# A fused recurrence and long-convolution kernel: the input matrix loaded raw and transposed by transfers, its factor moved to the output matrix, exponentials on ScalarE, and a fixed order of all operations

## The chip, the cores and the metric

The kernel runs on one core of a Trainium2 chip. The metric is device time in microseconds (us) of the core; a time exceeds the profile's span by about 2 us. Engines are named as the profile names them: PE is TensorE's matmuls, PEld its weight loads, DVE is VectorE, ACT is ScalarE, POOL is GpSimd, SP is SyncE.

Every run is called fast or slow: slow when it is more than 1.5% above the fastest run of the same kernel in its round. Ratios use fast runs only. A profile is one execution.

## The reference

Two independent parts, written side by side into one output of 2048 rows and 1280 columns, bfloat16.

```python
# A: a diagonal complex recurrence, 640 states, 2048 steps
dt = exp(log_dt); Lam = Lambda_re + 1j*Lambda_im
Lam_bar = exp(dt * Lam)
B_bar = ((Lam_bar - 1) / Lam)[:, None] * (B_re + 1j*B_im)     # the factor G times B
h[t] = Lam_bar * h[t-1] + B_bar @ x[t]
y[t] = 2 * real(C @ h[t]) + x[t] * Dskip
# B: a short convolution of k with 4 taps, times v, then a long convolution
kv = (short convolution of k along time) * v                   # 2048 x 640
y = irfft(rfft(kv, 4096) * rfft(ssm_k, 4096))[:2048] + kv * ssm_D
out_B = q * y
```

The recurrence is linear in its input, so the factor `(Lam_bar - 1) / Lam` may be applied to B, as the reference writes it, or to C.

## The kernel before

The program is a list of 700-odd named operations, each with an estimated cost on every engine that may run it. A list scheduler inside the kernel's file picks the order at build time: among the ready operations it takes the one that can start first by its own cost figures, with a due time to break ties.

```python
class Graph:
    SEM = 0.12
    ...
    def schedule(self, slots, ordered_tags, free_tags):
        ...
        while len(out) < n:
            best = None
            for o in ready:
                ...                                   # buffers free? engines free?
                for e, c in o.alts.items():           # every engine that may run it
                    ...
                    cand = (s, o.due, fin, o.idx, o, e, c, pick, td)
                    if best is None or self.better(cand, best, free):
                        best = cand
```

The powers of part A's start: e to the power of an argument is taken on GpSimd. `rn` holds the moduli of seven powers of `Lam_bar`, and the factor, the sets (`M_n`, block-diagonal 128-wide matrices made from them) and B's product all follow from it.

```python
        small("dtb", lambda: g.tensor_tensor(out=dt_b[:], in0=ecol[:, 0, :], in1=lpar[:, 0, :], op=ALU.pow), ["lam", "nrowf"], ["dt_b"], 0.4, "POOL")
        ...
        small("rn", lambda: g.tensor_tensor(out=rn[:], in0=ecol[:], in1=rn[:], op=ALU.pow), ["nrho"], ["rn"], 0.6, "POOL")
```

B is multiplied by the factor's set and so also transposed, in 50 products ("bb"). The large products ("dn", the bulk of part A) then take x against it, at full width. C is transposed by 100 products against an identity ("ct").

```python
            def f(e, blk=blk, pt=pt):                       # bb
                P = self.P(pt)
                for q, (j, k) in enumerate(blk):
                    self.nc.tensor.matmul(P[:, q // 4, 128 * (q % 4):128 * (q % 4) + 128],
                                          lhsT=bv(j // 5)[:, j % 5, 128 * k:128 * k + 128], rhs=self.mgv()[:, j, :], start=True, stop=True)
            ...
            def f(e, b=b):                                  # dn
                P = self.P(pt)
                for k in range(5):
                    nc.tensor.matmul(P[:, b, :], lhsT=self.BbT[:, j, k, :], rhs=self.xT[:, k, hf, 2 * b:2 * b + 2, :]
                                     .rearrange("p s m -> p (s m)"), start=(k == 0), stop=(k == 4))
```

Part B goes in five groups of 128 columns. For each, k and v come by DMA transposes on SyncE, the short convolution runs on VectorE, its result goes out to memory ("kvs") and is read back in another layout ("kvl", tile `kvd`), then two product stages, a pointwise part, two inverse stages ("i2", "i1") with one SBUF-to-SBUF transpose ("zt") between them, and the multiplication by q ("ob").

## Time and profile before

| | before |
|---|---|
| time | 249.55 us median of 3 runs (249.28 to 251.15) |
| span of the profile | 247.7 us |
| PE busy | 197.6 us, 80% |
| DVE busy | 181.0 us, 73% |

The first lines of the page: the span, busy time with its share, and the span in 40 slices of 6.2 us, each digit a busy share in tenths. PEclk is the clock that TensorE was granted, as far as the trace has records of it: they begin at 33.2 us here, and PEclk reads full up to its first record.

```profile
span 247.7 us, 8544 instructions
...
PE 197.6 (80%) x3843; PEld 139.3 (56%) x3857; DVE 181.0 (73%) x283; ACT 134.0 (54%) x164; POOL 37.6 (15%) x52
...
PE   0001688799999999889999749689979998999593
...
PEclk9999999999999999999999976999999999999999
...
```

PE does nothing in the first three slices, and is nearly full from 50 us on. The one dip that PEclk shows (slices 23 and 24, counted from 0) goes with the dip of PE in slices 22 and 23.

What PE waited for, the longest first (line of the waiting product, what released it: us in all, times, longest):

```profile
...
PE ps L672 <- DVE s L445: 21.2, 2, 20.9
PE ps L957 <- issue: 3.5, 2, 3.2
PE ps L1087 <- DMA s<-s: 3.0, 1, 3.0
...
```

What VectorE waited for, and the operation it waited for (the tile view: its duration in ns, then its start in us):

```profile
...
DVE rc L393 <- POOL rn L365: 10.2, 1, 10.2
...
```

```profile
...
L365 POOL TENSOR_TENSOR rn<-ecol,rn x1: 11567/11567/11567, 7.9 to 7.9; 128x70 f32<-128x70 f32 x1
...
```

Read together: the first useful products (line 672, B by its factor) start 20.9 us late. The wait names a VectorE operation, but VectorE itself stood still for 10.2 us, until one GpSimd power of 11.6 us was done. The first large product in the timeline (start, duration):

```profile
...
37.64 2.10 PE L702 MATMUL ps<-xT,BC 128*128 128x512 bf16 x8
```

Busy time of each engine by stretch (us, with the number of instructions):

```profile
...
core 0: us, PE busy (x) PEld busy (x) DVE busy (x) ACT busy (x) POOL busy (x), PEclk, DMA share, GB/s
0.00:24.00 24.00, 0.75 (x6) 0.61 (x7) 10.19 (x53) 4.24 (x8) 21.52 (x29) 1.00 0.88 178
24.00:50.00 26.00, 20.19 (x484) 16.67 (x485) 25.37 (x37) 22.96 (x26) 4.52 (x5) 1.00 0.84 159
50.00:90.00 40.00, 39.48 (x651) 23.54 (x653) 37.26 (x55) 25.16 (x34) 0.71 (x2) 1.00 0.58 114
...
```

From 24 to 90 us VectorE is nearly full (25.37 of 26, 37.26 of 40), and PE has done 20.9 us of work by 50 us. The groups of the large products and of B's products (count, busy us, mean ns):

```profile
...
L702 PE MATMUL ps<-xT,BC 128*128 128x512 bf16 x186 | 45.9, 380 | 1.5 <-ACT s L249 0.7
...
L672 PE MATMUL ps<-s,s 128*128 128x128 bf16 x50 | 4.8, 261 | 21.4 <-DVE s L445 21.2
...
```

14 of the 200 large products have no record in this trace, so their busy time is a little more than it shows.

### The profile page before, as it was taken

Reading aid. Unit: us, or ns where it says so; the run is one execution under the profiler, and the core shown is the slowest. Engines: PE = TensorE matmul, PEld = TensorE weight load, DVE = VectorE, ACT = ScalarE, POOL = GpSimd, SP = SyncE. Lnnn points to the kernel's source line nnn. Section 1 sums busy time; section 2 is a strip of 40 time slices with the busy share of each in tenths; the row PEclk is TensorE's granted clock in tenths of the full one; section 3 lists DMA queues with packets and bytes.
Section 4 is the critical chain, followed back from the end, with each engine's and each line's share of the span. In section 5 each row is a group of like instructions: output and inputs, shape, how many; then the busy total and the mean of one; then the engine's idle time right before and its main releaser. Section 6 shows DMA issues by size and latency. Waiting matters only on the chain.

```text
span 247.7 us, 8544 instructions
## 1 busy us (share of the span) xinstructions
PE 197.6 (80%) x3843; PEld 139.3 (56%) x3857; DVE 181.0 (73%) x283; ACT 134.0 (54%) x164; POOL 37.6 (15%) x52
## 2 busy tenths in 40 slices
PE   0001688799999999889999749689979998999593
PEld 0001575655655765547555628567757775777472
DVE  5408999999999899998868968763999557661110
ACT  2400999796674367775466746555257516652121
POOL 8896010500000010000011100001030110000000
PEclk9999999999999999999999976999999999999999
DMA  5997599494019496487494990554769494006414
GB/s 152 227 180 139 123 192 194 129 204 95 4 21 232 109 174 150 86 116 199 107 210 100 257 224 26 156 81 110 176 165 156 160 208 103 29 29 140 112 56 111
DMA packets 86695, 33.73 MB, mean 136 GB/s; under 512 B 82018, under 2 KB 84450, under 8 KB 86658
## 3 DMA queue, kind: packets, MB, share of 16 engines
q1 hardware_dynamic: 84916, 26.72, 55.3%
q0 software_dynamic: 1712, 6.46, 10.2%
q8 instruction: 30, 0.49, 0.8%
q14 instruction: 7, 0.06, 0.1%
q10 hardware_dynamic: 30, 0.00, 0.0%
HBM read 12.47 MB, written 7.86 MB: 82 GB/s over the span
## 4 chain that ended last, share of the span: by engine, by line
PE 57%; DVE 18%; POOL 7%; DMA 6%; ACT 6%; issue 4%; SPq 0%; DVEq 0%; ACTq 0%; POOLq 0%
PE ps L854 16%; PE ps L702 13%; PE ps L993 7%; PE ps L957 6%; DVE s L1016 5%; PE ps L1087 5%; POOL rn L365 5%; DMA s<-s 3%; DVE s L932 3%; DMA s<-in_B_k_dram 3%; ACT s L249 2%; DVE s L926 2%; PE ps L1049 2%; PE ps L803 2%; PE ps L858 2%
## 5 line engine op out<-in xcount | busy, mean ns | idle before, releaser
L249 ACT CAST s<-ps 128x1024 bf16<-128x1024 f32 x79 | 76.8, 1021 | 25.8 <-PE ps L993 12.0
L702 PE MATMUL ps<-xT,BC 128*128 128x512 bf16 x186 | 45.9, 380 | 1.5 <-ACT s L249 0.7
L854 PE MATMUL ps<-BC,hb 128*128 128x320 bf16 x240 | 36.4, 300 | 0.0
L251 DVE CAST s<-ps 128x1024 bf16<-128x1024 f32 x21 | 25.5, 1223 | 12.9 <-PE ps L993 8.1
L249 ACT CAST yo<-ps 128x640 bf16<-128x640 f32 x16 | 11.1, 692 | 37.3 <-PE ps L858 28.9
L957 PE MATMUL ps<-R,s 64*64 64x128 bf16 x1280 | 24.5, 228 | 6.8 <-issue 3.5
L702 PEld LDWEIGHTS <-BC 128*128 128x128 bf16 x200 | 18.8, 98 | 19.9 <-issue 1.0
L957 PEld LDWEIGHTS <-s 64*64 64x64 bf16 x1280 | 21.0, 113 | 12.9 <-issue 12.3
L854 PEld LDWEIGHTS <-hb 128*128 128x128 bf16 x240 | 21.9, 98 | 8.6
L1016 DVE TENSOR_TENSOR s<-s,s 128x1024 bf16<-128x1024 bf16 (+1 forms) x30 | 25.0, 866 | 0.8 <-DVE s L251 0.2
L993 PE MATMUL ps<-s,Wre 128*64 128x128 bf16 x320 | 22.4, 231 | 2.2 <-ACT s L249 1.8
L993 PEld LDWEIGHTS <-Wre 128*64 128x64 bf16 x320 | 19.4, 116 | 8.0 <-issue 6.3
L807 DVE TENSOR_TENSOR hb<-ps,hb 128x512 bf16<-128x512 f32 x30 | 19.6, 685 | 5.8 <-PE ps L803 5.7
L1094 DVE TENSOR_TENSOR s<-ps,s 128x1024 bf16<-128x1024 f32 x10 | 12.0, 1219 | 15.5 <-PE ps L1087 15.1
L249 ACT CAST hb<-ps 128x768 bf16<-128x768 f32 x19 | 15.3, 805 | 14.2 <-PE ps L702 12.8
L993 PE MATMUL ps<-s,Wim 128*64 128x128 bf16 x320 | 22.1, 228 | 0.0
L672 PE MATMUL ps<-s,s 128*128 128x128 bf16 x50 | 4.8, 261 | 21.4 <-DVE s L445 21.2
L993 PEld LDWEIGHTS <-Wim 128*64 128x64 bf16 x320 | 19.6, 116 | 0.0
L932 DVE TENSOR_TENSOR s<-s,s 128x2048 bf16<-128x2048 bf16 x15 | 18.4, 1224 | 0.4
L672 PEld LDWEIGHTS <-s 128*128 128x128 bf16 x50 | 4.2, 118 | 21.8 <-issue 21.8
L926 DVE TENSOR_SCALAR s<-s,sk 128x2048 bf16<-128x2048 bf16 x20 | 14.8, 750 | 0.4
L1087 PE MATMUL ps<-Ct,s 128*64 128x64 bf16 x640 | 12.3, 200 | 3.0 <-DMA s<-s 3.0
(156 smaller groups left out, 291.4 us busy)
## 6 DMA issues: line engine op xcount, KB each, us to landing
s<-kvd SPq DMA_DIRECT2D x5, 512.0 KB, 4.1
out_dram<-s SPq DMA_DIRECT2D x10, 256.0 KB, 4.1
out_dram<-yo SPq DMA_DIRECT2D x14, 160.0 KB, 2.9
s<-in_B_ssm_k_dram POOLq DMA_DIRECT2D x4, 512.0 KB, 7.0
kvd<-s SPq DMA_DIRECT2D x4, 512.0 KB, 2.6
s<-in_B_q_dram SPq DMA_DIRECT2D x6, 256.0 KB, 5.1
s<-in_B_q_dram POOLq DMA_DIRECT2D x4, 256.0 KB, 5.3
s<-in_A_x_dram SPq DMA_DIRECT2D x1, 960.0 KB, 5.3
```

What stands on the lines that cost most here:

```text
L249: self.nc.scalar.copy(out=out, in_=in_)
L251: self.eng[e].tensor_copy(out=out, in_=in_)
L365: small("rn", lambda: g.tensor_tensor(out=rn[:], in0=ecol[:], in1=rn[:], op=ALU.pow), ["nrho"], ["rn"], 0.6, "POOL")
L702: nc.tensor.matmul(P[:, b, :], lhsT=self.BbT[:, j, k, :], rhs=self.xT[:, k, hf, 2 * b:2 * b + 2, :] .rearrange("p s m -> p (s m)"), start= ...
L807: v.tensor_tensor(out=hv(r), in0=self.P(p2)[:, 0, :].rearrange("p (h m) -> p h m", h=2), in1=hv(r), op=ALU.add)
L854: nc.tensor.matmul(P[:, part, 0:320], lhsT=hap(j), rhs=self.CT[:, j, c0:c0 + 320], start=(j == 0), stop=False)
L926: v.tensor_scalar_mul(out=out, in0=k(j), scalar1=self.sk[:, G, j:j + 1])
L932: op(f"ca{j}{G}{h}", {"DVE": dve_tt(W_)}, lambda e, c=c, tt=tt: v.tensor_tensor(out=c(), in0=c(), in1=tt(), op=ALU.add), r=[f"tm{G}{h}"], ...
L957: nc.tensor.matmul(P[64 * ri:64 * ri + 64, r, 128 * b4:128 * b4 + 128], lhsT=d[64 * r:64 * r + 64, 4 * qd + b4, a0, :], rhs=self.R[64 * r: ...
L993: nc.tensor.matmul(P[64 * pi:64 * pi + 64, ri, 128 * k4:128 * k4 + 128], lhsT=W[:, kp, pi, :], rhs=A[:, kp + 16 * pi, :], start=True, stop ...
L1016: v.tensor_tensor(out=o, in0=a, in1=b, op=op_)
L1087: nc.tensor.matmul(P[64 * ah:64 * ah + 64, b // 8, 64 * (b % 8):64 * (b % 8) + 64], lhsT=Z[:, 16 * h + b, 64 * ri:64 * ri + 64], rhs=self. ...
```

## The change

Three things at once. The powers become exponentials on ScalarE, with one more load of the sine table placed early. B is loaded by four DMA transposes and used raw; the factor is applied to C, which comes by four DMA transposes too. And the scheduler is replaced by a fixed order with fixed engines for all operations, which a search over the whole program had found. The intent: the large products need only x and B, so they can start before the phases are ready, and the order fills what follows better.

```diff
-    SEM = 0.12
+    SEM = 0.06
@@ the order @@
+    def place(self, slots, text):
+        letter = {"P": "PE", "A": "ACT", "D": "DVE", "G": "POOL", "S": "SP"}
+        ...
+        for word in text.split():
+            name, _, e = word.partition("/")
+            o = ops[name]
+            o.eng = letter[e] if e else next(iter(o.alts))
+            ...
+ORDER = """
+ld_ldt ld_lre J0 consts J1 ... px1 ci1 ss ex0/A px2 px3 ex1/D px4 ex2/A dtap1/D s1h12
+ex3/A set_1_0/D B10 s1h10 set_3_0/D e1h12/A set_2_0/G s1h11 ... dn1_8_0 kvl0/G e1h03/A ... cv310/D q0/G ...
+... (721 names in all)
+"""
-        order = self.g.schedule({"8": self.N8, "4": self.N4, "P": 4, "Y": 2}, ("8", "4"), ("P", "Y"))
-        return order
+        self.slots = {"8": self.N8, "4": self.N4, "P": 4, "Y": 2}
+        return self.g.place(self.slots, ORDER)
@@ the exponentials @@
-        small("dtb", lambda: g.tensor_tensor(out=dt_b[:], in0=ecol[:, 0, :], in1=lpar[:, 0, :], op=ALU.pow), ["lam", "nrowf"], ["dt_b"], 0.4, "POOL")
+        small("dtb", lambda: s.activation(out=dt_b[:], in_=lpar[:, 0, :], func=ACT.Exp), ["lam"], ["dt_b"], 0.3, "ACT", due=-24)
-        small("rn", lambda: g.tensor_tensor(out=rn[:], in0=ecol[:], in1=rn[:], op=ALU.pow), ["nrho"], ["rn"], 0.6, "POOL")
+        def f_rn():
+            s.activation(out=rn[:], in_=rn[:], func=ACT.Exp)
+            s.activation(out=scr[:], in_=self.hpi[:], func=ACT.Sin)
+        small("rn", f_rn, ["nrho", "hpi"], ["rn"], 1.8, "ACT", due=-22)
@@ B raw: the 50 products and their evictions go; the large products at half width @@
+                    nc.sync.dma_start_transpose(out=self.BT[:, :, u, 320 * h:320 * h + 320], ...
-                    nc.tensor.matmul(P[:, b, :], lhsT=self.BbT[:, j, k, :], rhs=...)
+                    for ri in range(2):
+                        nc.tensor.matmul(P[64 * ri:64 * ri + 64, b, :], lhsT=self.BT[:, k, ri, 64 * j:64 * j + 64], rhs=...)
@@ C: 100 products against the identity become 40 against the factor's set @@
-                        nc.tensor.matmul(P[64 * h:64 * h + 64, q // 4, ...], lhsT=cv(h)[:, k, 64 * j:64 * j + 64], rhs=self.ident[:], ...)
+                            nc.tensor.matmul(self.P(pt)[:, u, 0:320], lhsT=self.M["G"][us, 2 * J + ri, :],
+                                             rhs=cv(ri)[us, J, 320 * b:320 * b + 320], start=(ri == 0), stop=(ri == 1))
@@ engines: sets may run on POOL, the convolution's scalings on ACT @@
-            mk_set(n, lambda i=i: ss[:, i, :, :], ["ss"], {"DVE": 0.85})
+            mk_set(n, 10, lambda i=i: ss[:, i, :, :], "ss", {"DVE": 0.85, "POOL": 2.2}, 2)
... (cost figures, signs of the sets, small tiles reused: left out)
```

In the order, a letter after the slash is the engine (A ScalarE, D VectorE, G GpSimd, S SyncE).

## The prediction

> **What bounds the kernel now.** The page's busy table gives PE 197.6 of 247.7 us (80%), DVE 181.0 (73%), ACT 134.0 (54%). Busy time by stretches shows three regimes:
> - 0 to 24 us: PE busy 0.75 us. The chain of waits runs through POOL: dt_b (2.0 us), then `rn`, a power on 128x70 elements that takes 11.57 us; DVE idles 10.2 us for it (waits view). Then come the factor, its set, W and the products of B. The first large product (line 702) starts at 37.6 (timeline).
> - 24 to 112 us: DVE is full (25.4 of 26, 37.3 of 40, 20.9 of 22); from 93 to 112 the chain lies mostly on DVE.
> - After 112: PE leads, with about 19 us of its idle time left: an issue gap of 3.2 us at 142, the second coarse step at 154 to 162, a transpose landing in 7.6 us at 224, the tail.
>
> PE work at its back-to-back pace in the timeline (5 of 512 columns 1.08 us; a half row of projection 1.5; 16 stage-two products 0.5; and so on) adds up to only about 181 us.
>
> **What changes.**
> 1. Both powers leave POOL (13.6 us in the chain). Instead: two exponentials on ACT (estimate 0.26 us each, as its other 70-wide operations) and two more table loads, 1.28 us each in the trace. [...] The phase chain should end near 12 us instead of 19.5.
> 2. The 50 products of B with its factor (3.4 us) and their 7 evictions go; B comes by four transposes (about 2.7 us of queue each, estimated from x's 16.1 us for 8). Large products then need only x and B: the first at 17 to 18 us instead of 37.6. C's 100 products (3.5 us) become 40, about 2.7 us; altogether 14 evictions (13 us) become 10 of 640 columns (0.69 each, 7 us).
> 3. Large products become 400 half-width ones instead of 200. Stage two (128x64) runs 64 of 128 columns in 1.98 us, 31 ns each, so pairs run side by side; I expect a pair of 512 columns to keep 216 ns. [...]
> 4. Some sets move to POOL, a few scalings (estimate 1.9 us against 0.75) to ACT; DVE's total stays near 180 us.
> 5. The fixed order spreads the projections between B's stages and puts 10 us of other PE work behind the last transposes.
>
> **Sum.** At 50 us, before has done about 16 us of dense PE work: a lag of 34. After should reach its first large product with a lag of 12: 20 us off the start on PE, though DVE's lag falls only from 14 to 7. PE: 12 lag + 181 dense with switches + 15 holes (PE and DVE are now equally loaded, and a fixed order slips) + 4 tail = 212 span; times exceed the span by 1.8.
>
> Predicted **214 us**, range **207 to 226**. Chances: faster 0.97, same 0.02, slower 0.01.
>
> **Signs.** The exponential under 0.5 us on ACT; first large product before 20 us; PE busy near 190 us, above 87% of the span; large products near 45 us busy in all (not 85); DVE above 80%; the late transpose wait gone.
>
> **What would make it wrong.** Half-width pairs not overlapping (+40 us); transposes slowed by other traffic, so that x's second half comes after 45 us; [...] holes of 25 us rather than 15 (about 225), or nearly none (about 205).

The sum came to 212 us of span, 214 of time. "With switches" stands for 1 to 2 us that I added for changes between forms of product, a cost that no trace shows.

## The result, and the profile after

| | before | after |
|---|---|---|
| time, same chip | 249.42 us median of 4 runs (249.04 to 251.15) | 237.49 us median of 4 runs (232.37 to 244.95) |
| fast runs | | 232.37, 232.81 |
| slow runs | | 242.17, 244.95 |
| span of the profile | 247.7 us | 230.8 us (a fast run) |
| mean granted clock of the profile, from its first record on | 0.986 | 0.963 |

A ratio is the mean time of one kernel's fast runs over that of the other's of the same rounds, so it is not quite the ratio of the medians above. Here it is 0.931 (95% interval 0.924 to 0.939): faster, but by 6.9%, not 14%, and half of the runs are slow ones. The median of 237.49 us lies outside the range on record, and so do the fast runs.

The same lines of the page, after:

```profile
span 230.8 us, 8736 instructions
...
PE 195.7 (85%) x3947; PEld 137.3 (59%) x3947; DVE 180.8 (78%) x279; ACT 140.7 (61%) x166; POOL 44.1 (19%) x67
...
PE   0619996979999999997659999659999999999953
...
PEclk9976999999999999999988999958999999999999
...
```

PE has work from slice 1 on (transposes of x), a hole in slice 2, and 9 tenths in slice 3, where it had 1 tenth before. It is busy for 1.9 us less in all. PEclk now has three dips, at slices 2 and 3, 20 and 21, and 26 and 27.

The exponentials in ScalarE's timeline (start, duration, line, operation):

```profile
...
8.37 0.21 ACT L430 ACTIVATE dt_b<-lpar 128x10 bf16<-128x10 f32 x1
9.17 0.26 ACT L445 ACTIVATE rn<-rn 128x70 f32<-128x70 f32 x1 [0.58 <-DVE rn L442]
9.43 1.28 ACT L446 ACT_TABLE_LOAD   x1
...
```

Both exponentials take under 0.3 us, and the table load 1.28 us, as predicted. The first large product, and the large products as a group:

```profile
...
20.89 1.49 PE L751 MATMUL ps<-xT,BC 128*64 128x512 bf16 x12
```

```profile
...
L751 PE MATMUL ps<-xT,BC 128*64 128x512 bf16 x400 | 47.4, 381 | 0.2 <-ACT s L331 0.2
...
```

400 products at half width have a mean of 381 ns and take 47.4 us of busy time, where 186 of the 200 at full width took 45.9: pairs of them run side by side, as predicted. The stretches, and what PE waited for:

```profile
...
core 0: us, PE busy (x) PEld busy (x) DVE busy (x) ACT busy (x) POOL busy (x), PEclk, DMA share, GB/s
0.00:24.00 24.00, 11.44 (x201) 9.07 (x203) 20.51 (x55) 14.57 (x22) 15.90 (x31) 0.86 1.04 194
24.00:50.00 26.00, 22.92 (x382) 13.17 (x378) 23.62 (x43) 19.30 (x25) 10.02 (x10) 1.00 1.06 181
50.00:90.00 40.00, 39.33 (x729) 24.57 (x728) 34.09 (x52) 29.74 (x35) 1.75 (x3) 1.00 0.56 100
...
```

```profile
...
PE ps L1132 <- DMA s<-s: 6.9, 4, 4.3
PE ps L1002 <- DVE s L924: 4.3, 1, 4.3
PE ps L703 <- DMA s<-in_A_x_dram: 4.1, 2, 3.9
PE ps L1002 <- issue: 2.7, 2, 2.2
...
```

PE has done 34.4 us of work by 50 us, 13.4 more than before. It had been meant to be about 22 further (a lag of 12 for one of 34). The 6.9 us of waits for line 1132 are inverse steps waiting for the transposes of their input, and one of them has a second price:

```profile
...
core 0: us, PE busy (x) PEld busy (x) DVE busy (x) ACT busy (x) POOL busy (x), PEclk, DMA share, GB/s
...
148.00:152.00 4.00, 0.03 (x1) 0.00 (x0) 1.78 (x2) 0.48 (x1) 0.00 (x0) 0.83 1.24 189
152.00:156.00 4.00, 3.68 (x71) 2.77 (x72) 1.19 (x2) 0.00 (x0) 0.00 (x0) 0.50 0.71 218
...
```

PE stood still from 148.0 to 152.3 us, and then worked at half clock (PEclk 0.50) until 157.5. Such stretches follow three holes (13.0 to 17.3, 118.4 to 120.6 and 148.0 to 152.3 us). A product takes about twice as long in them: ten of line 899 took 2.87 us at 154.6 us and 1.52 at 157.7, just after the third. So I count half of the busy time in them as lost: 1.8, 1.4 and 2.6 us, 5.8 in all, where the kernel before lost 3.1 after its one hole. In the trace's clock records the three stretches lasted 6.83, 3.41 and 6.83 us, and in the third PE was busy for 1.72 of the first 3.41 us and for all of the second. How long a hole it takes, and what ends a stretch, is not shown: the clock fell at 119.9 us, where PE had been busy for 1.47 of the 3.41 us before, and stayed whole after a wait of 2.2 us in r1_after_again.

PEclk misses a part of it, because the trace's clock records begin late. Products of one form (128 columns on the full array), in the timeline of the kernel before, on either side of its first record at 33.2 us (start, duration, count at the end):

```profile
...
23.79 1.87 PE L672 MATMUL ps<-s,s 128*128 128x128 bf16 x16 [20.85 <-DVE s L445]
...
33.18 1.52 PE L632 MATMUL ps<-ident,s 128*128 128x128 bf16 x24
...
```

That is 117 ns each, then 63 (107 and 56 from start to start). In the changed kernel the change from 107 to 55 lies between 10.3 and 12.4 us, and its first record is at 10.7. So I count PE's busy time up to the first record as half clock too: 7.3 us before (3.6 lost) and 4.2 after (2.1 lost). With these, half clock cost PE 6.8 us before and 7.8 after, and its work at full clock is 190.8 and 187.9 us.

One identity makes every profile comparable. With the PE work done by 50 us, the PE work in all, and PE's idle time after 50 us, read from the stretches,

span = (50 - work by 50) + work in all + idle after 50.

| kernel (profile) | span | 50 - PE busy by 50 us | PE busy in all | PE idle after 50 us |
|---|---|---|---|---|
| before | 247.7 | 29.1 | 197.6 | 21.1 |
| prediction | 212 | 12 | 181 | 19 |
| after | 230.8 | 15.6 | 195.7 | 19.4 |

So, of the 16.9 us that the fast profile gained, 13.4 come from the start, 1.9 from less PE time and 1.6 from fewer holes.

The prediction's row is in another unit, though: its lag and its 181 count dense work, at full clock. (It gives the kernel before a lag of 34, where this table has 29.1.) In its unit, with what half clock cost after 50 us put to the last column, the identity reads:

| kernel (profile) | span | 50 - full-clock work by 50 us | full-clock work in all | idle, or lost to half clock, after 50 us |
|---|---|---|---|---|
| before | 247.7 | 32.7 | 190.8 | 24.2 |
| prediction | 212 | 12 | 181 | 19 |
| after | 230.8 | 19.5 | 187.9 | 23.4 |
| r3_exp_only | 254.7 | 33.2 | 188.9 | 32.6 |
| r3_new_greedy | 249.8 | 25.9 | 191.9 | 31.9 |
| r4_loads_sp_again | 227.2 | 18.5 | 187.0 | 21.7 |
| r4_pow_back | 236.3 | 27.2 | 186.9 | 22.3 |
| r4_sets_dve | 227.3 | 18.2 | 186.5 | 22.6 |

The change gained 13.2 us at the start, 2.9 of PE work and 0.8 after 50 us. The miss of 18.8 us against the predicted span is 7.5 at the start, 6.9 of PE work and 4.4 of holes and half clock: all three terms were too small. In the four profiles of the fixed order in this table (the kernel after and three of the r4 runs) the work is nearly constant (186.5 to 187.9 us), while PE's busy time runs from 193.0 to 197.5: that difference is nearly all half clock.

### The profile page after: what moved, and what is told of

It reads as the page before. It is cut to its first block, busy times and chain, and to the rows that moved or that the text cites. A ratio compares the mean times of both kernels' runs of the same rounds, so it can differ in the third digit from the quotient of the medians.

```text
span 230.8 us, 8736 instructions
## 1 busy us (share of the span) xinstructions
PE 195.7 (85%) x3947; PEld 137.3 (59%) x3947; DVE 180.8 (78%) x279; ACT 140.7 (61%) x166; POOL 44.1 (19%) x67
## 5 line engine op out<-in xcount | busy, mean ns | idle before, releaser
L331 ACT CAST s<-ps 128x1024 bf16<-128x1024 f32 x81 | 78.4, 1020 | 26.0 <-PE ps L1002 12.9
L751 PE MATMUL ps<-xT,BC 128*64 128x512 bf16 x400 | 47.4, 381 | 0.2 <-ACT s L331 0.2
L899 PE MATMUL ps<-BC,hb 128*128 128x320 bf16 x240 | 38.1, 307 | 1.9 <-issue 1.7
L751 PEld LDWEIGHTS <-BC 128*64 128x64 bf16 x400 | 21.5, 110 | 18.0 <-issue 2.0
L899 PEld LDWEIGHTS <-hb 128*128 128x128 bf16 x240 | 22.6, 100 | 12.4 <-issue 2.4
L333 DVE CAST s<-ps 128x1024 bf16<-128x1024 f32 x19 | 22.8, 1220 | 6.0 <-PE ps L1002 4.4
L331 ACT CAST yo<-ps 128x640 bf16<-128x640 f32 x11 | 7.6, 691 | 28.8 <-PE ps L903 19.3
L1038 PE MATMUL ps<-s,Wre 128*64 128x128 bf16 x320 | 21.1, 221 | 0.4 <-issue 0.2
L331 ACT CAST hb<-ps 128x768 bf16<-128x768 f32 x17 | 13.5, 798 | 8.0 <-PE ps L751 8.0
L1132 PEld LDWEIGHTS <-s 128*64 128x64 bf16 x640 | 11.7, 117 | 10.1 <-DMA s<-s 7.6
L912 POOL DMA_DIRECT2D out_dram<-yo x6 | 3.4, 573 | 72.5 <-ACT yo L331 37.3
L1061 DVE TENSOR_TENSOR s<-s 128x1024 bf16<-128x1024 bf16 x20 | 13.8, 688 | 0.3
```

The source lines that it names most:

```text
L331: self.nc.scalar.copy(out=out, in_=in_)
L333: self.eng[e].tensor_copy(out=out, in_=in_)
L751: nc.tensor.matmul(P[64 * ri:64 * ri + 64, b, :], lhsT=self.BT[:, k, ri, 64 * j:64 * j + 64], rhs=self.xT[:, k, hf, 2 * b:2 * b + 2, :].re ...
L899: nc.tensor.matmul(P[:, part, 0:320], lhsT=hap(j), rhs=self.CT[:, j, c0:c0 + 320], start=(j == 0), stop=False)
L1038: nc.tensor.matmul(P[64 * pi:64 * pi + 64, ri, 128 * k4:128 * k4 + 128], lhsT=W[:, kp, pi, :], rhs=A[:, kp + 16 * pi, :], start=True, stop ...
L1061: v.tensor_tensor(out=o, in0=a, in1=b, op=op_)
```

## The experiments

Sixteen runs. All results were correct. The records call the theories by letters in places: A is the half clock after holes, B that the clock falls for another cause, E is a clash of two GpSimd-issued loads with transposes.

### First round: the state, the clock, the start

**r1_after_again**: no edit, the changed kernel once more on the chip of this round.

> The changed kernel once more, as the yardstick for the three runs beside it. Fast runs near 232.6 us as before; if the slow runs (242 and 245 us at granted clocks of 0.94 and 0.92) are a property of this kernel, some of these will be slow again; if they were an accident of the first chip, none will.

Measured: 238.9 us median of 6 runs: 228.23 and 229.8 at one end, 242.69, 244.07 and 244.66 at the other, and 235.11 between them. Ratio of the fast runs 0.918 (0.910 to 0.925). So the kernel has two states by itself, some 14 us apart, and more slow than fast runs. In its profile (fast, 227.7 us) the wait for the transposes at 147.8 us was 2.2 us instead of 4.3, and no half clock came after it.

**r1_warm_filler**: 18 useless products ahead of the inverse step `i120`, in the PSUM tile it overwrites, to keep PE busy in the hole.

```diff
+                if G == 2 and h == 0:
+                    for _ in range(18):
+                        nc.tensor.matmul(P[:, 0, :], lhsT=self.ident[:], rhs=self.xT[:, 0, 0, 0:2, :]..., start=True, stop=True)
```

> Only 18 useless products of 512 columns are put in front of the late-transpose products of the third group, into the same PSUM tile that those products overwrite, so that TensorE has work in the 4.3 us in which it waits for that transpose (148.0 to 152.3 us in the profile). Theory A [...]: no half-clock stretch at 151 to 157.7 us, 2.5 to 3 us less time, about 229.8 us against 232.6. Theory B [...]: the half-clock stretch stays or moves, time the same within 0.5 us or longer.

Measured: 242.15 us median (236.89 to 244.86); the profile fell in a slow run. The clock stayed whole after the fillers, but the time can't be judged: no run was near the fast state. What the slow profile gave is where a slow run parts from a fast one. PE waited for the reload of the first group's convolution result:

```profile
...
PE ps L1004 <- DMA s<-kvd: 6.7, 1, 6.7
...
```

(after, fast: 0.7 us at that place). Two stretches of the fast profile of the changed kernel, with the transfers' share and GB/s in the last columns, and then the same two stretches of the slow run:

```profile
...
core 0: us, PE busy (x) PEld busy (x) DVE busy (x) ACT busy (x) POOL busy (x), PEclk, DMA share, GB/s
...
48.00:52.00 4.00, 2.69 (x113) 1.92 (x117) 1.92 (x3) 1.77 (x3) 0.00 (x0) 1.00 0.98 182
52.00:56.00 4.00, 3.90 (x121) 3.24 (x111) 3.96 (x5) 2.99 (x4) 0.00 (x0) 1.00 0.64 135
...
```

```profile
...
48.00:52.00 4.00, 0.61 (x10) 0.22 (x4) 1.23 (x1) 0.94 (x2) 0.00 (x0) 1.00 1.31 81
52.00:56.00 4.00, 0.72 (x28) 0.72 (x32) 0.00 (x0) 0.00 (x0) 0.00 (x0) 0.56 1.05 122
...
```

From 37 to 40.4 us the issues on the two queues agree to 0.1 us. Then GpSimd's queue starts the reload `kvl0` (and at 44.7 us the load `q0`), while SyncE's queue is running the two transposes of W. In the fast run PE goes on at 49.2 us, in the slow one at 55.3: the engines are busy all the while (share 1.31 and 1.05 in the slow run) but move 81 GB/s where the fast run moves 182. All of the later program is shifted. The fast run issues the same loads beside the same transposes at the same times, so the overlap alone does not decide it.

**r1_late_i120**: `i120` and its successor moved later in the order, behind `d02_0`, so that the transposes have time to land.

```diff
- ... e1h33/A d01_9 i120 cm30 d01_3 ... py0_02 ob20 ... d02_3 d02_0 d01_5 ...
+ ... e1h33/A d01_9 cm30 d01_3 ... py0_02 ... d02_3 d02_0 i120 ob20 d01_5 ...
```

> Only the order is changed: the products that wait for the third group's late transpose come five TensorE operations later (two projection halves and three small products go ahead of them, about 4 us of work). If the wait at 148 to 152.3 us is what cost the time there, the wait goes, and with it the half clock after it: 4 us plus about 3 us, about 226 us. If VectorE or the transfers are the real limit behind it, the wait comes back elsewhere and the time falls by less than 2 us.

Measured: 237.47 us median (231.18 to 241.31), slow profile, one fast run of six. The slow state covers the gain that was asked for.

**r1_start**: the tap addition `dtap1` moved up before the evictions of x, and the eviction `ex1` to ScalarE, which takes the 4.3 us wait of line 1002 away.

```diff
- trig px0 ... px3 ex1/D px4 ex2/A dtap1/D s1h12
+ trig dtap1/D px0 ... px3 ex1/A px4 ex2/A s1h12
```

> Only the order at the start is changed: the second eviction of x goes to ScalarE, which was idle from 14.2 us, instead of VectorE, and the tap addition of the second filter goes ahead of the scaling of the sets. Now stage one's products wait from 13.0 to 17.3 us for these, and then run at half clock until 20.9. If that wait is the limit: stage one begins near 14 us at full clock, the first large product near 16.5 instead of 20.9 us, total 3 to 5 us less, about 228.5 us. If VectorE is the true limit of the first 100 us, the gain is used up there and the total falls by less than 1.5 us.

Measured: 239.7 us median, ratio of the fast runs 0.930 (0.922 to 0.939), no gain over the changed kernel's 0.918. The first large product came at 16.98 us instead of 20.89 (the profile is a slow run, but slow runs part from fast ones only after 40 us), but PE then waited for an eviction on VectorE at 38 us:

```profile
...
PE ps L761 <- DVE hb L335: 4.3, 1, 4.3
...
```

VectorE reached that eviction at 37.16 us, where it had reached it at 37.37. So at the start PE is not what limits: making it 3.9 us earlier buys nothing while VectorE's queue is as long as before.

### Second round: the reload on SyncE's queue

Theory E says that the slow runs come from loads issued by GpSimd that run beside transposes on SyncE's queue. Moved to SyncE, they go out in order with the transposes (in r2_load_sp_warm SyncE issues the reload at 39.80 us and the transposes of W at 40.30 and 44.77).

**r2_load_sp**: `kvl0` from GpSimd to SyncE, after the last transpose of x and before those of W.

```diff
- ... e1h02/D dn1_8_0 kvl0/G e1h03/A ... s2h12 x131 m1_0_0 ...
+ ... e1h02/D dn1_8_0 e1h03/A ... s2h12 x131 kvl0/S m1_0_0 ...
```

> Only one transfer is issued otherwise: the reload of the first convolved group (from DRAM, ahead of stage one) goes out from SyncE, before the two W transposes, instead of from GpSimd. In the profiles of fast runs of the changed kernel TensorE waits 0 to 0.7 us for that reload at 48 us, in the three profiles of slow runs 6.7 to 8.1 us, with everything before it the same; after the long wait the clock is halved for some 5 us. Theory C (the slow runs of this kernel are this one transfer landing late): no run above 236 us, median about 230 to 233 instead of 238.9, clock above 0.96 in all. Rival D (the slow runs are a state of the chip, a lower clock that comes from outside): half of the runs stay above 238 us.

Measured: 231.84 to 239.02 us in five runs, and one outlier of 477.3 us, the profiled one, with PE busy 97% of the time; that execution ran PE slowly throughout and says nothing of the edit. Median 235.7, ratio 0.936 (0.930 to 0.941). The longest runs are gone, but runs of 236 to 239 stayed.

**r2_load_sp_warm**: the same, with the 18 fillers.

> The same with the 18 useless products ahead of the third group's late-transpose products. Theory A [...]: where the run beside it has the half clock after 150 us, this has none; 1 to 3 us less than without the filler where the gap is long[...]. Theory B (the clock falls for another cause): no difference in clock.

Measured: 238.64 us median (233.5 to 242.61), ratio 0.937: again no gain from fillers. The slow profile shows no wait for the reload, but another one, at 53.2 to 62.5 us:

```profile
...
PE ps L1040 <- issue: 9.3, 1, 9.3
...
```

"issue" is a wait for nothing that the profile shows. `q0` was still on GpSimd, issued at 44.7 us beside the transposes, and while PE stood still the DMA engines moved 50 to 146 GB/s. I read this as the clash holding up whatever transfer comes next; that is a guess from this one trace, which does not show that PE waited for a transfer at all.

**r2_load_sp_late**: the reload on SyncE, with the later `i120`.

> The reload from SyncE, and the third group's late-transpose products five TensorE operations later. If the wait at about 148 us costs what it shows, 2 to 4 us less than the reload alone, and up to 3 us more where its half clock goes; if the wait comes back elsewhere because another engine is full, less than 1 us.

Measured: 230.95 us median (228.67 to 237.23), ratio 0.922 (0.918 to 0.926). Two runs of six are slow by the rule (237.23 and 234.43). That is 1.4 points under r2_load_sp, as hoped, but no better than r3_loads_sp below, which leaves `i120` where it was; so the gain is not shown to be `i120`'s.

**r2_load_sp_start**: the reload on SyncE, all sets on VectorE, small tables later on GpSimd, and the edits of r1_start.

> The reload from SyncE, and the start rearranged so that GpSimd no longer stretches VectorE: all sets on VectorE (five move, 0.82 us each), the phase table's integer work on GpSimd after the first sets, the second eviction of x on ScalarE, the tap addition earlier. In the changed kernel VectorE's small operations between 10 and 31 us are stretched by about 8 us in all while GpSimd computes (a 64x70 cast 2.3 us, sets 1.8 us instead of 0.8). If that stretching limits the start: the first convolution ends near 32 us instead of 36.4, and the total falls by 2 to 4 us. If not: within 1 us.

Measured: 229.09 us median (226.89 to 235.35, one run slow), ratio 0.915 (0.911 to 0.919). Two of its edits are tried alone or nearly so in r1_start and r4_sets_dve.

### Third round: both loads, and the parts of the change alone

**r3_loads_sp**: only `kvl0` and `q0` moved to SyncE, nothing else.

```diff
- kvl0/G  (as above)     - q0/G
+ kvl0/S  after x131     + q0/S
```

> The changed kernel with the reload of the first convolved group and the load of the first group's q issued from SyncE, behind which the transposes of W and v queue up in order, instead of from GpSimd. In the slow profiles a GpSimd transfer in flight together with transposes makes both crawl (51 to 104 GB/s at a full DMA share for some ten us, against 145 to 336 in the fast profile), and whatever TensorE needs next comes 7 to 9 us late: once the reload[...]. Theory E (this overlap is the slow state): no run above 237 us, median 230 to 233. Rival D (the slow state comes from outside the program): runs above 238 remain as with the reload alone.

Measured: 230.79 us median, 6 runs from 228.86 to 232.21: no slow run. Ratio 0.923 (0.919 to 0.927), the same as the changed kernel's fast runs. So the slow runs go when these two loads leave GpSimd's queue, and the fast ones stay as they were. It takes 7 to 8 us off the median and explains no part of the miss between 212 and 230 us. The changed kernel itself was not run on this chip; but here r2_load_sp and r2_load_sp_warm, with `q0` still on GpSimd, had runs of 236 to 243 us. (The expectation's 145 to 336 GB/s are the fast profile's 47 to 50 us; from 42 to 52 us it moved 73 to 336.)

**r3_best**: both loads on SyncE, the later `i120`, the sets on VectorE, the small tables later, and the start's edits.

> All changes of order that gained: both loads from SyncE, late-transpose products five operations later, start rearranged with all sets on VectorE. If the gains of the separate runs add (about 4 us for the later products, about 6 for the start, counted against the reload alone at 235.7): median 225 us, no slow runs, clock above 0.965. If they share one cause: 228 to 229.

Measured: 227.39 us median (225.06 to 229.38; two runs, 228.45 and 229.38, count as slow), ratio 0.906 (0.901 to 0.911). It beats both kernels, and lies between the two expectations.

**r3_exp_only**: the kernel before, with the exponentials on ScalarE, under its own scheduler. Nothing else of the change.

```diff
-        small("dtb", lambda: g.tensor_tensor(... op=ALU.pow), ["lam", "nrowf"], ["dt_b"], 0.4, "POOL")
+        small("dtb", lambda: s.activation(out=dt_b[:], in_=lpar[:, 0, :], func=ACT.Exp), ["lam"], ["dt_b"], 0.3, "ACT", due=-24)
-        small("rn", lambda: g.tensor_tensor(... op=ALU.pow), ["nrho"], ["rn"], 0.6, "POOL")
+        small("rn", f_rn, ["nrho", "hpi"], ["rn"], 1.8, "ACT", due=-22)    # f_rn: Exp, then a Sin to load the table
```

> The kernel before with its two powers replaced by exponentials on ScalarE and nothing else; its list scheduler orders the rest. The power of 11.6 us leaves the chain at the start, so the scaling of the sets can begin near 12 us instead of 19.5. If the start is what bounds: 6 to 8 us less, about 243 us. If the greedy order spends it on waits for B or VectorE: less than 3 us.

Measured: 257.6 us median of 4 runs (256.49 to 258.37), ratio 1.032 (1.028 to 1.037): slower than before, against an expectation of about 243. PE's longest waits:

```profile
...
PE ps L677 <- DMA s<-in_A_B_im_dram: 12.7, 1, 12.7
PE ps L637 <- DMA s<-in_A_x_dram: 7.2, 1, 7.2
...
```

B's products begin at 15.5 us instead of 23.8, but wait for B itself, and then the second half of x comes late (29.8 us). The first large product starts at 34.98 us, only 2.7 before the old 37.64. With other times and cost figures the scheduler also made another order of everything later. By the second table of the identity, the start gained nothing (33.2 us for 32.7), and the time after 50 us lost 8.4 us to holes and half clock.

**r3_new_greedy**: the changed kernel with all its new arithmetic, but the order made by the old scheduler.

```diff
-        return self.g.place(self.slots, ORDER)
+        return self.g.schedule(self.slots, ("8", "4"), ("P", "Y"))
```

> All new arithmetic (raw turned B, factor in C, exponentials), but the old list scheduler instead of the fixed order. If the arithmetic brings the gain: about 233 us. If the fixed order brings it: 240 to 246 us, because the scheduler's settings were tuned for the kernel before and its cost figures are short of the measured ones.

Measured: 253.64 us median of 4 runs (251.53 to 255.9), ratio 1.013 (1.008 to 1.018): no gain at all.

```profile
...
PE ps L1002 <- DVE R L586: 9.5, 1, 9.5
PE ps L1132 <- DMA s<-s: 8.7, 3, 4.8
...
```

By the second table, the start is 6.8 us better than before, and 7.7 us more after 50 us lose it. Subtracted from each other, the ratios 1.013 and 0.918 to 0.931 say that the fixed order, with its choice of engines, is worth 8 to 10 points over this scheduler with this arithmetic, and the arithmetic nothing under it. The scheduler was not tuned anew for the changed kernel, so a better one might have used the arithmetic.

### Fourth round: what was still open

All on one chip, with r3_loads_sp as the base, since it has no slow runs.

**r4_loads_sp_again**: the base.

> The changed kernel with the two early GpSimd loads on SyncE once more, as the base of the three others on the same chip. Expected 229 to 232 us with no run above 234, if the slow runs of the changed kernel come from these two loads; if they were absent by luck last time, runs of 236 to 245 come back.

Measured: 230.31 us median, 228.64 to 233.09, ratio 0.921 (0.915 to 0.927). Two runs (233.03 and 233.09) lie 1.9% above the fastest, so they count as slow by the rule, but none comes near the 242 to 245 us of the changed kernel, and none is above 234. With r3_loads_sp that makes 12 runs without the old slow state.

**r4_pow_back**: the powers back on GpSimd, in the fixed order.

```diff
-        small("dtb", lambda: s.activation(... func=ACT.Exp), ["lam"], ["dt_b"], 0.3, "ACT", due=-24)
+        small("dtb", lambda: g.tensor_tensor(out=dt_b[:], in0=scr[:, 0:1].to_broadcast([128, 10]), in1=lpar[:, 0, :], op=ALU.pow), ["lam", "nrowf"], ["dt_b"], 0.4, "POOL")
-            s.activation(out=rn[:], in_=rn[:], func=ACT.Exp)
-            s.activation(out=scr[:], in_=self.hpi[:], func=ACT.Sin)
+            g.tensor_tensor(out=rn[:], in0=scr[:]..., in1=rn[:], op=ALU.pow)
```

> The base with the two powers back on GpSimd in place of the exponentials, the fixed order unchanged. If the exponentials are worth their 11 to 13 us of the chain inside the fixed order: 240 to 244 us. Rival (the start of the changed kernel is set by VectorE's work and by the arrival of x, and only part of the chain shows): 232 to 236 us.

Measured: 238.39 us median (237.49 to 240.94), ratio 0.956 (0.951 to 0.961), so 8.1 us more than the base's median, between the two expectations. The power and PE's wait:

```profile
...
L450 POOL TENSOR_TENSOR rn<-scr,rn x1: 11543/11543/11543, 8.4 to 8.4; 128x70 f32<-128x70 f32 x1
...
```

```profile
...
PE ps L707 <- ACT xT L333: 11.2, 1, 11.2
...
```

The wait names ScalarE's eviction of x, because in the fixed order the evictions stand behind the sines, the sines need phases from GpSimd, and those stand behind the power in GpSimd's queue. The first large product starts at 28.95 us instead of 20.54. By the second table, 8.7 of the 9.1 us of span lie at the start (27.2 us for 18.5). Inside this order the exponentials are worth 8.1 of the 13 us by which `rn` and `dt_b` became shorter (11.5 and 2.0 us against 0.26 and 0.21); r3_exp_only shows them worth less than nothing in the other.

**r4_warm**: 14 fillers ahead of each of two inverse steps that wait for transposes.

```diff
+                if h == 0 and G in (0, 2):
+                    for _ in range(14):
+                        nc.tensor.matmul(P[:, 0, :], lhsT=self.ident[:], rhs=self.xT[:, 0, 0, 0:2, :]..., start=True, stop=True)
```

> The base with 14 useless 512-column products ahead of the inverse steps of the first and third column groups, in the holes where TensorE waits 3.6 and 3.7 us for transposes. Theory A (half clock after a hole costs time by itself): no half clock after these holes, about 3 us of PE busy time saved there (14 fillers add some 6 us to it), and the time 1.5 to 4 us under the base (ratio to it 0.983 to 0.993). Rival (the lost pace is made up before the next wait, which ends the same): half clock gone, time within 0.7 us of the base. If the fillers hold up the real product, 1 to 3 us more.

Measured: 234.24 us median (229.78 to 237.17), but four of the six runs are slow by the rule, and two of the base's. The fast runs alone give 0.926 (0.918 to 0.934) and 0.921 (0.915 to 0.927): no gain, and no clear loss. The stretches about the second hole, first of the base, then of this run:

```profile
...
core 0: us, PE busy (x) PEld busy (x) DVE busy (x) ACT busy (x) POOL busy (x), PEclk, DMA share, GB/s
146.00:150.00 4.00, 1.61 (x52) 1.20 (x51) 2.54 (x3) 1.27 (x2) 0.00 (x0) 0.98 1.19 266
150.00:154.00 4.00, 4.00 (x45) 2.50 (x42) 1.82 (x2) 0.12 (x1) 0.00 (x0) 0.60 0.74 143
...
```

```profile
...
146.00:150.00 4.00, 3.91 (x22) 1.77 (x20) 2.40 (x3) 1.13 (x2) 0.00 (x0) 1.00 1.53 186
150.00:154.00 4.00, 2.85 (x78) 2.31 (x79) 1.29 (x2) 0.00 (x0) 0.00 (x0) 1.00 0.77 230
...
```

The half clock after that hole is gone (1.00 for 0.60), and the inverse step takes 1.20 us instead of 1.53. But by 158 us PE stood at about the same place (157.80 and 158.18 us for the next step of the kind): in this execution the transposes landed 1.9 us later. After that the run lost 2.8 us of span more, 1.6 of it in an "issue" gap of 3.0 us (1.4 in the base). PE's busy time without its 6.4 us of fillers is 194.5 us, more than the base's 193.0, because half clock came in other places: from 110.1 to 113.5 and from 215.9 to 219.3 us, so that after its first records this run has as much half clock as the base (13.65 us each). Theory A holds for the clock at the second hole. What a run with less half clock in all would take, it doesn't test. Why four of the runs were slow stays open.

**r4_sets_dve**: all sets on VectorE.

```diff
- set_2_0/G set_2_1/G set_12_0/G set_4_1/G set_12_1/G set_G_0/G
+ set_2_0/D set_2_1/D set_12_0/D set_4_1/D set_12_1/D set_G_0/D
```

> The base with every set of columns on VectorE, none on GpSimd. If GpSimd's sets and VectorE's operations hold each other up at the start: VectorE's mean set falls from 1.12 to about 0.8 us, its busy time to 50 us changes little, and the time is 1 to 3 us lower. Rival (the stretched operations cost nothing, moving the sets adds their own time to VectorE, which is full to 36 us): 1 to 4 us more than the base.

Measured: 229.22 us median (228.26 to 231.68), ratio 0.920 (0.915 to 0.925): the same as the base. VectorE's sets up to 50 us, in the base and here:

```profile
...
L518 DVE TENSOR_TENSOR M<-E,ss 128x640 bf16<-128x640 bf16 x6 | 6.8, 1166 | 0.0
...
```

```profile
...
L518 DVE TENSOR_TENSOR M<-E,ss 128x640 bf16<-128x640 bf16 x11 | 8.6, 818 | 0.0
...
```

VectorE made 11 sets in 8.6 us where it had made 6 in 6.8: the mean falls from 1166 to 818 ns once GpSimd does none beside it; by what mechanism is not shown. Five sets moved to GpSimd had taken only 1.8 us off VectorE. PE is busy 2.6 us more by 50 us and 4.5 us more in all, but that is half clock: counted as above, it cost 11.0 us here and 6.1 in the base (here the clock records begin, and the pace doubles, only at 22.7 us; PEclk reads 1.00 over the first 24 us, where the base has 0.86). By the second table the two runs agree within 1 us in every term, and in time.

## Why the prediction was wrong

The direction was right, and so were most of the signs: exponentials under 0.3 us, half-width pairs side by side, large products at 47.4 us. The size was wrong. The step that failed is this one: "PE: 12 lag + 181 dense with switches + 15 holes + 4 tail = 212 span". In the same unit, full-clock work, the trace has 19.5 + 187.9 + 23.4. The sum was never tried on the kernel that was already measured: with the prediction's own numbers for it, 34 of lag, 181 and about 19 of idle time left, it gives 234 us, 14 short of 247.7.

1. **"181 dense" measured 187.9 us at full clock,** and 195.7 of busy time. The 181 was a sum of the best pace of each kind of product, as blocks in the timeline ran it. It stands under "What bounds the kernel now" and is used unchanged for the kernel after. The kernel before already showed that PE doesn't hold that pace: its page said 197.6 busy, 190.8 without the half clock. The products removed did save about what was said: 2.9 us, for some 4 less the 1 to 2 of the term. The prediction's own sign, "PE busy near 190", contradicts its sum; with 190 in it the sum is 221.
2. **"12 lag" measured 19.5.** The start gained 13.2 us on PE, not 20. The first large product came at 20.89 us instead of 17 to 18, because PE waited 4.3 us for a tap addition on VectorE, and its lag was 16.4 us there; the rest came by 50 us. But r1_start removed that wait and gained nothing, since VectorE's queue to 38 us was as long as before. The prediction had written that VectorE's lag falls by 7 us only, and then counted PE's 20.
3. **Holes: 15 + 4 predicted, 23.4 measured:** 19.4 idle, as predicted in sum, and 4.0 lost to half clock, for which there was no term. The transposes that were to have time now still held up PE for 6.9 us. The sign "the late transpose wait gone" was wrong.
4. **The slow runs were not foreseen.** Half of the runs are 10 to 12 us longer, which lifts the median from about 232.6 to 237.5. r3_loads_sp and r4_loads_sp_again, with two loads moved from GpSimd's to SyncE's queue, had none of that kind in 12 runs. That it takes these loads on GpSimd's queue is shown, as far as 12 runs can. Why the same overlap is harmless in the other half of the runs, and by what mechanism the two queues then get only 81 GB/s out of busy engines, is not; nor whether the queue matters or only the order in which the transfers go out.
5. **The cause of the gain was put in the wrong place.** The prediction credits nearly everything to the powers and to the raw B. With the old scheduler the powers' removal costs 3.2%, and the whole new arithmetic gains nothing (1.013). In the fixed order moving the powers is worth 8.1 us. Only with the fixed order, engines included, did an earlier start become an earlier end.
6. **What PE time at half clock is worth.** I had no term for it, and it cost PE 7.8 us, 2.1 of them where PEclk reads full. But it is an account of where PE's time is, and not shown to be time that can be had: r4_sets_dve lost 11.0 us to it and the base 6.1, in the same time; r3_best, the fastest kernel, lost 10.4 in its profile. Where PE had work earlier, at half clock, it filled what had been idle time. r4_warm moved the half clock and did not reduce it.

What stays open: the 6.9 us of pace (which product loses how much, and where, was not taken apart), the slow runs of r4_warm, the mechanism of the clash, and how much of the fixed order's 8 to 10 points is order and how much its choice of engines.

## What to carry to other kernels

When you add up a bound engine's time, start from its measured busy time in the profile and subtract what the change removes; a sum of best paces was about 8% short of it here for both kernels (181 us for 197.6 and 195.7). Try the whole sum on the known kernel before you use it on the new one. Check the clock by the duration of one form of product, not by PEclk alone (107 ns a product here where PEclk read full, 56 at full clock). Before crediting a shorter chain at the start, ask which engine's queue is full just after it (VectorE's was), and whether the order of the rest can use the earlier start: the same exponentials gave −8.1 us in one order and +7.5 us in another. If a kernel's times fall into two clumps, compare a fast and a slow trace for the first instant at which they differ; here that was one load issued beside transposes, and moving two loads to the transposes' own queue removed the slow clump.
